# Projecting queries and keys of the sliding-block layers unpadded, through HBM, and setting constants later

## The chip, the cores and the metric

One core of one Trainium2 chip. The metric is the device time of one execution in microseconds (us); a kernel's time is the median of its runs. PE is the matmul engine, PEld its weight load, DVE VectorE, ACT ScalarE, POOL GpSimd, SP the engine from whose queue (SPq) most transfers are issued.

## The reference, cut to what matters

```python
# x: 1 x 2048 x 640; H = 32 heads of 20; W = 256
def _A_ref(x, wqkv, wo):                      # sliding-block attention
    qkv = (x @ wqkv).reshape(B, S, 3, H, Dh)...
    scores = einsum("bhqd,bhkd->bhqk", q, k) * (Dh ** -0.5)
    mask = (idx[:, None] - idx[None, :] >= 0) & (idx[:, None] - idx[None, :] < W)
    p = softmax(where(mask, scores, -1e9)); o = p @ v
    return o.transpose(...).reshape(B, S, D) @ wo
# _B_ref is the same without a mask: full attention
x = x + _A_ref(_layernorm(x), A_wqkv, A_wo)   # layer 1 (l = 0 in the code)
x = x + _B_ref(_layernorm(x), B_wqkv, B_wo)   # layer 2 (l = 1)
x = x + _A_ref(_layernorm(x), A_wqkv, A_wo)   # layer 3 (l = 2)
x = x + _B_ref(_layernorm(x), B_wqkv, B_wo)   # layer 4 (l = 3)
```

## The kernel before

The rows are cut into 4 chunks of 512, the heads into 8 groups of 4. A head has 20 columns, and the program computes its scores from a strip of 32 partitions of its own. The kernel had two ways to get there. The full layers (`l % 2 == 1`) project five blocks of 128 unpadded columns per chunk for queries and for keys, store them to HBM, and load each head's 20 rows back onto its strip. The sliding-block layers used weights with 12 zero columns after every 20, so that the projection itself lands on the strips; that takes eight projections instead of five, but no trip through HBM.

A scheduler in the program emits all engines' instructions "tile" by tile (a tile is one ScalarE exponential over two or three score banks); between tiles it advances waiting tasks (projections, normalization, statistics) by their need.

```python
def get_w(l, n, c, i):                       # weights of one projection
    t = wqkp.tile([P, KD, P], BF16, name="wqk", tag="wqk")
    wtick[l, n, c, i] = state["tick"] + 4     # may be used 4 tiles later
    if l % 2:                                 # full layer: unpadded, from the input
        a = n * D + i * P
        nc.sync.dma_start(out=t[:], in_=wq_view[1][:, :, a : a + P])
        return t
    d = wqk_d[i][:, n * KD * P : (n + 1) * KD * P]
    if l == 0 and c == 0:                     # pad once on chip, keep a copy in HBM
        ...
        nc.sync.dma_start(out=d, in_=t[:]...)
    else:
        nc.sync.dma_start(out=t[:]..., in_=d)
    return t

def t_qk_window(l, c, g):                     # sliding: straight onto the strips
    ...
    yield from project(wt, xnT[l, c], lambda: q[:])
    ...
    yield from project(wt, xnT[l, c], lambda: k[:])
    ready.add(("qk", l, c, g))

def t_full(l, n, c, b):                       # full: one block of 128, to HBM
    wt = yield from take_w(l, n, c, b)
    yield from project(wt, xnT[l, c], staged) # evicted into one of 4 staging tiles
    nc.sync.dma_start(out=dst, in_=staging.pop())
    ready.add(("qk"[n], l, c, b))
...
def keep_clock(least):                        # fillers
    while state["heat"] < least:
        t = choose(False)
        if t is not None and state["credit"] > -0.5:
            state["credit"] -= advance(t)     # real work first
            continue
        ...
        nc.tensor.matmul(ps[:, b, :], lhsT=ident[:], rhs=masks[:, 0, :], ...)
        state["heat"] += 1.0
...
def t_stats0(c):                              # layer 1's statistics of chunk c
    for i in range(4):
        stats(0, c, i)
        yield ("pe", 0.1)
    ready.add(("x", 0, c))
```

At the start, before any work:

```python
for t in (wop, *kts, *qts):                   # tiles whose unused rows must be zero
    nc.vector.memset(t[:], 0.0)
...
with tc.manual_schedule():
    other_constants()
    push("stats", t_stats0(0), 0, 0.4)
    push_layer(0, 0)
    require(("qk", 0, 0, 0))
```

The softmax here doesn't subtract the row's maximum and nothing guards it: scores larger than these inputs give would overflow.

Of the kernel before, what the change touches and what calls it, by code (L numbers as in the profile page):

```python
# [14 lines left out]
P = 128  # L15
# [6 lines left out]
G = 8  # L22
# [3 lines left out]
SCALE = DH ** -0.5  # L26
HD = D // 2
VW = DH + 1

PARTS = {  # L30
    l: [(e[n], e[n + 1]) for n in range(len(e) - 1)]
# [5 lines left out]
def kernel(  # L37
# [16 lines left out]
        return ctx.enter_context(tc.tile_pool(name=name, bufs=bufs, **kw))  # L54

    big = pool("big", 1)
    wqkp = pool("wqkp", 9)
    kvp = pool("kvp", 3)
    qap = pool("qap", 3)
    kap = pool("kap", 18)  # L60
    vap = pool("vap", 10)
    xtp = pool("xtp", 5)
    onp = pool("onp", 2)
# [26 lines left out]

    kts = [big.tile([P, S], BF16, name=f"kt{n}", tag=f"kt{n}") for n in range(3)]
    qts = [big.tile([P, C], BF16, name=f"qt{n}", tag=f"qt{n}") for n in range(4)]

    ps = psp.tile([P, 8, C], F32, name="ps", tag="ps")
    op = ps[:, 7, :]


    wqk_d = dram.tile([G, P, 2 * KD * P], BF16, name="wqk_d", tag="wqk_d")
    k_d = {l: dram.tile([D, S], BF16, name=f"k_d{l}", tag=f"k_d{l}") for l in (1, 3)}
    q_d = {l: dram.tile([NC, D, C], BF16, name=f"q_d{l}", tag=f"q_d{l}") for l in (1, 3)}  # L100
    v_d = {l: dram.tile([P, G, NT * 4 * VW], BF16, name=f"v_d{l}", tag=f"v_d{l}") for l in (1, 3)}

    wq_view = [w.rearrange("(c p) f -> p c f", p=P) for w in wqkv_in]
# [10 lines left out]
        for j in range(4):  # L114
            nc.sync.dma_start(out=wop[32 * j : 32 * j + DH, :, :], in_=v[j])

    for t in (wop, *kts, *qts):
        nc.vector.memset(t[:], 0.0)
    nc.gpsimd.memset(ident[:], 0.0)
    nc.gpsimd.affine_select(  # L120
        out=ident[:], in_=ident[:], compare_op=ALU.not_equal, fill=1.0,
# [2 lines left out]
    nc.gpsimd.memset(nhalf[:], -0.5)  # L124

    def other_constants():
        load_wop(0)
        nc.vector.memset(op, 0.0)
        nc.vector.tensor_copy(
            out=sel4[:], in_=ident[:].rearrange("p (j m) -> p j m", j=4)[:, :, DH]  # L130
        )

        sp32 = rzp.tile([32, 2, 16], BF16, name="sp32", tag="sp32")
        nc.vector.tensor_copy(
            out=sp32[:], in_=ident[0:32, 0:32].rearrange("p (n r) -> p n r", n=2)
        )
        sp16 = rzp.tile([32, 16], BF16, name="sp16", tag="sp16")
        nc.vector.tensor_tensor(out=sp16[:], in0=sp32[:, 0, :], in1=sp32[:, 1, :], op=ALU.add)
        nc.vector.tensor_copy(
            out=spread4[:].rearrange("p q (j m) -> p (q j) m", m=32),  # L140
            in_=sp16[:].unsqueeze(2).to_broadcast((32, 16, 32)),
        )

        nc.gpsimd.memset(masks[:], 1.0)
        for m, b, ge in (
            (2, 0, True), (2, 2, False), (2, 3, True),
            (0, 0, False), (0, 1, True), (0, 3, False),
            (1, 1, False), (1, 2, True),
        ):
            v = masks[:, m, b * P : (b + 1) * P]  # L150
            nc.gpsimd.affine_select(
                out=v, in_=v, compare_op=ALU.is_ge if ge else ALU.is_gt, fill=0.0,
                base=0, pattern=[[1 if ge else -1, P]], channel_multiplier=-1 if ge else 1,
            )
# [22 lines left out]
    def push(name, gen, need, left):  # L177
        lead = 0
        if type(name) is tuple and need <= first_use(1, NC - 1, 0):

            chain = {"out": True, "ln": name[1] == 1, "v": name[1] == 1 and name[-1] == 0}
            chain["k"] = chain["q"] = name[-1] == 0
            lead = 5 * chain.get(name[0], False)
        insort(todo, Task(name, gen, need, left, lead))

# [74 lines left out]


    live = Counter()
    cap = {"qa": 3, "ka": 18, "va": 10, "xnT": 5, "kt": 3, "vt": 3, "qt": 4, "ln": 1, "w": 4, "vs": 2}

    def room(*tags):
        while any(live[t] + tags.count(t) > cap[t] for t in tags):
# [24 lines left out]
    def get_w(l, n, c, i):  # L291

        t = wqkp.tile([P, KD, P], BF16, name="wqk", tag="wqk")
        wtick[l, n, c, i] = state["tick"] + 4
        if l % 2:
            a = n * D + i * P
            nc.sync.dma_start(out=t[:], in_=wq_view[1][:, :, a : a + P])
            return t
        d = wqk_d[i][:, n * KD * P : (n + 1) * KD * P]
        if l == 0 and c == 0:  # L300
            tv = t[:].rearrange("p c (j m) -> p c j m", j=4)
            nc.gpsimd.memset(tv[:, :, :, DH:32], 0.0)
            src = raw[:, :, n * D + 80 * i : n * D + 80 * (i + 1)]
            nc.vector.tensor_copy(
                out=tv[:, :, :, 0:DH], in_=src.rearrange("p c (j e) -> p c j e", j=4)
            )
            nc.sync.dma_start(out=d, in_=t[:].rearrange("p c m -> p (c m)"))
            wtick[l, n, c, i] = 0
        else:
            nc.sync.dma_start(out=t[:].rearrange("p c m -> p (c m)"), in_=d)  # L310
        return t

    def take_w(l, n, c, i):
# [46 lines left out]
    def t_ln(l, c):  # L360
# [3 lines left out]
        for n in (1, 0):  # L364
            order = worder[l, n]
            if order and not any(e in wtiles for e in order):
                wtiles[order[0]] = get_w(*order[0])
        users[l, c] = (9, 12, 9, 11)[l]
        mv = mvs.pop((l, c))
        rstd = lnp.tile([P, 4], F32, name="rstd", tag="rstd")  # L370
        nc.gpsimd.tensor_scalar(
# [89 lines left out]
    vt = {}  # L461
    qt = {}

    def t_qk_window(l, c, g):
        while ("xnT", l, c) not in ready:
            yield ("wait", 1)
        yield from room("qa", "ka", "w", "w")
        wt = yield from take_w(l, 0, c, g)
        q = qap.tile([P, C], BF16, name="qa", tag="qa")
        yield from project(wt, xnT[l, c], lambda: q[:])  # L470
        wt = yield from take_w(l, 1, c, g)
        k = kap.tile([P, C], BF16, name="ka", tag="ka")
        yield from project(wt, xnT[l, c], lambda: k[:])
        live["w"] -= 2
        qa[c, g], ka[c, g] = q, k
        used(l, c)
        ready.add(("qk", l, c, g))

    def t_full(l, n, c, b):

        while ("xnT", l, c) not in ready:
            yield ("wait", 1)
        yield from room("w")
        wt = yield from take_w(l, n, c, b)
        yield from project(wt, xnT[l, c], staged)
        rows = slice(b * P, (b + 1) * P)
        dst = k_d[l][rows, c * C : (c + 1) * C] if n else q_d[l][c, rows, :]
        nc.sync.dma_start(out=dst, in_=staging.pop())
        live["w"] -= 1
        used(l, c)  # L490
        ready.add(("qk"[n], l, c, b))
# [64 lines left out]
    def push_layer(l, c):  # L556
# [3 lines left out]
        if l % 2:  # L560
            halves = ((0,), (1,)) if l == 1 else ((0, 1),)
            for h in halves:
                push(("v", l, c, *h), t_v(l, c, h), need[4 * h[0]], 2.8 * len(h))
            for b in range(KD):
                g = b * P // 80
                for n in (1, 0):
                    worder[l, n].append((l, n, c, b))
                    first = need[g] if n else index[l, c, g, PARTS[l][0] if c == 0 else None]
                    push(("qk"[n], l, c, b), t_full(l, n, c, b), first, 1.1)
            return  # L570
        for g in range(G):
            for n in (0, 1):
                worder[l, n].append((l, n, c, g))
            push(("qk", l, c, g), t_qk_window(l, c, g), need[g], 2.2)
            if g == 0:
                push(("v", l, c), t_v(l, c, (0, 1)), need[0], 5.6)

# [80 lines left out]
                units.append(small.popleft())  # L658
    units += [Unit(3, 0, g, PARTS[3][1]) for g in range(G)]
    units += [Unit(3, c, g) for c in range(1, NC) for g in range(G)]  # L660
    full = [u for u in units if not u.windowed]
    place = {id(u): n for n, u in enumerate(full)}
    index = {(u.l, u.c, u.g, u.part): n for n, u in enumerate(units)}

    def first_use(l, c, g):
# [2 lines left out]
            return index[l, c, g, None]  # L668
        return next(index[l, 0, g, p] for p in PARTS[l] if 4 * c < p[1])

    def load_unit(u):

        l, c, g = u.l, u.c, u.g
        key = (l, c, g)
        k0, k1 = key_blocks(l, u.part)
        live["vt"] += 1
        vt[key] = kvp.tile([P, NT * 4 * VW], BF16, name="vt", tag="vt")
# [3 lines left out]
        )  # L681
        live["kt"] += 1
        live["qt"] += 1
        kt[key] = kts[len(loaded) % 3]
        qt[key] = qts[len(loaded) % 4]
        for j in range(4):
            rows = slice((4 * g + j) * DH, (4 * g + j + 1) * DH)
            strip = slice(32 * j, 32 * j + DH)
# [3 lines left out]

    def unit_needs(u):
        l, c, g = u.l, u.c, u.g
        if u.windowed:
            return [("qk", l, c, g)]
        k0, k1 = key_blocks(l, u.part)
        chunks = range(k0 // 4, k1 // 4)
        blocks = range(80 * g // P, (80 * g + 79) // P + 1)
        return [("q", l, c, b) for b in blocks] + [  # L700
            n
            for cc in chunks
# [5 lines left out]
    def ensure_loaded(u, force):  # L708
# [3 lines left out]
        if force:  # L712
            for n in needs:
                require(n)
        elif any(n not in ready for n in needs) or any(
            live[t] >= cap[t] for t in ("kt", "vt", "qt")
        ):
            return
        load_unit(u)
# [2 lines left out]
    def start_unit(u):  # L722
        for n in unit_needs(u):
            require(n)
        if not u.windowed:
            ensure_loaded(u, True)

    def load_ahead():

        for u in full:  # L730
            if id(u) not in loaded:
                ensure_loaded(u, False)
                return

    part_o = {}

# [26 lines left out]
    def s_emitted(u):  # L763
        if u.windowed:
            live["qa"] -= 1
            live["ka"] -= (u.c > 0) + (u.c == NC - 1)
        else:
            live["kt"] -= 1
            live["qt"] -= 1
# [55 lines left out]
        ready.add(("x", 0, c))  # L825

    with tc.manual_schedule():
        other_constants()
        push("stats", t_stats0(0), 0, 0.4)
        push_layer(0, 0)  # L830
        require(("qk", 0, 0, 0))

        def narrow(u):
# [163 lines left out]
```

## Time and profile before

| before | us |
|---|---|
| median of 4 runs | 2437.43 |
| lowest, highest | 2426.58, 2444.76 |
| span of the profiled run | 2436.6 |

The score matmuls (5504, the same in every kernel) serve as a ruler: a stage runs from one score matmul to another, whatever else lies between. "Half clock" is the time in which the throttle granted PE half its speed, summed from the clock records of the trace; it is the finer form of the mean clock that a view by stretches shows.

| stage, by scores | what runs | length before, us |
|---|---|---|
| to the first | start | 24.8 |
| first to 272nd | layer 1 alone | 127.6 |
| 272nd to 944th | layer 1, woven with early parts of layer 2 | 275.8 |
| 944th to 1088th | its last part | 71.7 |
| 1088th to 4000th | layers 2 and 4, layer 3 in between ("middle") | 1232.2 |
| 4000th to the end | layer 4 | 704.5 |

"The early stage" means first to 944th score from here on.

### The profile page before, as it was taken

What the parts mean: (1) busy time and instruction counts of PE and PEld (TensorE: products, weight loads), DVE (VectorE), ACT (ScalarE), POOL (GpSimd) and SP (SyncE); (2) the same over time, 40 slices, a digit from 0 to 9 for tenths busy, and PEclk for the clock granted to TensorE, in tenths of its full rate; (3) what the DMA queues carried; (4) which work ended last, traced back from release to release, by engine and by line L of the source; (5) the groups of instructions that cost most, each with busy time, mean ns of one, the idle gap of its engine ahead of it and who ended that gap; (6) DMA issues with size and microseconds to landing.
All of it is one profiled execution on the core that took longest, in us unless ns stands there. A gap on an engine that the chain in (4) does not pass through costs nothing.

```text
span 2436.6 us, 38927 instructions
## 1 busy us (share of the span) xinstructions
PE 2030.6 (83%) x15811; PEld 742.4 (30%) x15811; DVE 870.4 (36%) x1966; ACT 2234.2 (92%) x1779; POOL 39.8 (2%) x112
## 2 busy tenths in 40 slices
PE   6889899988888898888889888888877777777777
PEld 2333333323322333333322333332222222222222
DVE  6767767423323344433353434542200010001001
ACT  5878788899999999999998999999999999999997
POOL 2000000000000000000000000000000000000000
PEclk8999999999988999989997899999755575557556
DMA  4113223222100222102320032122100010010100
GB/s 149 58 43 83 64 61 91 54 75 75 47 24 26 48 66 67 39 13 56 83 67 16 16 89 74 31 46 62 58 28 26 25 36 26 25 36 31 33 13 12
DMA packets 141124, 120.19 MB, mean 49 GB/s; under 512 B 66064, under 2 KB 129680, under 8 KB 140944
## 3 DMA queue, kind: packets, MB, share of 16 engines
q1 hardware_dynamic: 140944, 117.70, 17.8%
q8 instruction: 124, 2.03, 0.3%
q14 instruction: 56, 0.46, 0.1%
HBM read 96.40 MB, written 21.23 MB: 48 GB/s over the span
## 4 chain that ended last, share of the span: by engine, by line
ACT 44%; PE 31%; issue 14%; DVE 10%; DMA 1%; SPq 0%; POOL 0%; ACTq 0%; DVEq 0%
ACT pt L903 44%; PE ps L337 8%; PE ps L889 7%; PE ps L953 4%; PE ps L510 4%; PE ps L588 3%; DVE pt L935 3%; PE ps L428 3%; DVE oT L760 1%; PE ps L392 1%; DVE st L283 1%; DVE ka L283 1%; DVE on L810 1%; DVE qa L283 1%; PE ps L806 1%
## 5 line engine op out<-in xcount | busy, mean ns | idle before, releaser
L903 ACT ACTIVATE pt<-ps 128x1536 bf16<-128x1536 f32 (+2 forms) x1704 | 2198.8, 1518 | 155.6 <-PE ps L889 132.3
L889 PE MATMUL ps<-qt,kt 32*128 32x512 bf16 x4096 | 667.7, 464 | 262.5 <-ACT pt L903 249.5
L953 PE MATMUL ps<-pt,vt 128*21 128x512 bf16 x4096 | 489.7, 465 | 11.1 <-DVE oT L760 7.6
L889 PEld LDWEIGHTS <-kt 32*128 32x128 bf16 x4096 | 202.1, 94 | 679.0 <-issue 656.8
L935 DVE TENSOR_TENSOR pt<-pt,masks 128x1024 bf16<-128x1024 bf16 (+5 forms) x403 | 240.4, 625 | 165.0 <-ACT pt L903 164.3
L337 PE MATMUL ps<-xnT,wqk 128*128 128x512 bf16 x1040 | 284.2, 400 | 16.8 <-DVE st L283 2.9
L760 DVE CAST oT<-ps 128x512 bf16<-128x512 f32 x112 | 76.8, 686 | 389.1 <-PE ps L953 389.0
L953 PEld LDWEIGHTS <-vt 128*21 128x21 bf16 x4096 | 106.2, 90 | 326.7 <-issue 316.5
L588 PE MATMUL ps<-masks,ident 128*128 128x512 bf16 x627 | 191.8, 419 | 11.9 <-DVE rz L787 3.0
L510 PE MATMUL ps<-wop,on 128*128 128x320 bf16 x968 | 174.5, 322 | 5.3 <-DVE x_sb L519 3.9
L810 DVE TENSOR_TENSOR on<-oT,ps 128x512 bf16<-128x512 bf16 x128 | 87.8, 686 | 153.2 <-PE ps L806 148.0
L889 PE MATMUL ps<-qa,ka 32*128 32x384 bf16 (+2 forms) x1408 | 118.1, 278 | 26.3 <-ACT pt L903 23.3
L519 DVE TENSOR_TENSOR x_sb<-x_sb,ps 128x320 bf16<-128x320 bf16 x120 | 58.0, 483 | 218.0 <-PE ps L510 217.7
L337 PEld LDWEIGHTS <-wqk 128*128 128x128 bf16 x1040 | 90.0, 100 | 140.8 <-issue 70.6
L428 PE MATMUL ps<-wv,xnT 128*128 128x320 bf16 x640 | 109.6, 303 | 4.0 <-DVE va L283 1.0
L510 PEld LDWEIGHTS <-on 128*128 128x128 bf16 x968 | 89.9, 103 | 73.6 <-issue 38.6
L953 PE MATMUL ps<-pt,va 128*21 128x384 bf16 (+2 forms) x1408 | 79.2, 291 | 21.7 <-DVE oT L760 16.0
L283 DVE CAST st<-ps 128x512 bf16<-128x512 f32 x78 | 53.9, 691 | 116.8 <-PE ps L337 111.0
L588 PEld LDWEIGHTS <-ident 128*128 128x128 bf16 x627 | 55.7, 103 | 96.4 <-issue 66.6
L799 DVE COPY rT<-ps 32x128 bf16<-32x128 bf16 x128 | 26.9, 210 | 143.3 <-PE ps L797 142.7
L787 DVE RECIPROCAL rz<-ps 128x16 f32<-128x16 f32 x128 | 32.7, 256 | 114.5 <-PE ps L782 113.5
L889 PEld LDWEIGHTS <-ka 32*128 32x128 bf16 x1408 | 40.1, 92 | 96.3 <-issue 91.0
(59 smaller groups left out, 778.8 us busy)
## 6 DMA issues: line engine op xcount, KB each, us to landing
wqk<-wqk_d SPq DMA_DIRECT2D x112, 160.0 KB
vt<-v_d SPq DMA_DIRECT2D x48, 336.0 KB
kt<-k_d SPq DMA_DIRECT2D x192, 80.0 KB
wqk<-in_B_wqkv_dram SPq DMA_DIRECT2D x80, 160.0 KB
qt<-q_d SPq DMA_DIRECT2D x384, 20.0 KB
v_d<-vs SPq DMA_DIRECT2D x16, 336.0 KB
k_d<-st SPq DMA_DIRECT2D x40, 128.0 KB
q_d<-st SPq DMA_DIRECT2D x40, 128.0 KB
```

Of the source, the lines that this page charges most:

```text
L283: nc.vector.tensor_copy(out=out_, in_=in_)
L337: nc.tensor.matmul(pq, lhsT=wt[:, dc, :], rhs=xt[:, dc, :], start=(dc == 0), stop=(dc == KD - 1),)
L428: nc.tensor.matmul(pv, lhsT=xt[:, dc, i * P : (i + 1) * P], rhs=wv_sb[l % 2][:, dc, h * HD : (h + 1) * HD], start=(dc == 0), stop=(dc == K ...
L510: nc.tensor.matmul(yp, lhsT=on[:, g, qb * P : (qb + 1) * P], rhs=wop[:, g, i * HD : (i + 1) * HD], start=(last or g == 0), stop=(g == G - 1),)
L519: nc.vector.tensor_tensor(out=xv, in0=had, in1=yp, op=ALU.add)
L588: nc.tensor.matmul(ps[:, b, :], lhsT=ident[:], rhs=masks[:, 0, :], start=True, stop=True)
L760: nc.vector.tensor_copy(out=oT[:], in_=op)
L810: nc.vector.tensor_tensor(out=on[:, g, :], in0=oT[:], in1=zb, op=ALU.mult)
L889: nc.tensor.matmul(sp[:, i, col * P : (col + qn) * P], lhsT=u.k(kc, j), rhs=u.q(j, q0, qn), start=True, stop=True,)
L903: nc.scalar.activation(out=pt[:, i:k, b0 * P :], in_=sp[:, i:k, b0 * P :], func=ACT.Exp, scale=SCALE,)
L935: nc.vector.tensor_tensor(out=pt_[:, i:k, b0 * P :], in0=pt_[:, i:k, b0 * P :], in1=mv_, op=ALU.mult,)
L953: nc.tensor.matmul(op[32 * j : 32 * j + VW, q0 * P : (q0 + qn) * P], lhsT=u.v(kc, j), rhs=pt[:, i, col * P : (col + qn) * P], start=(first ...
```

## The change

The sliding-block layers get their queries and keys as the full layers do, five unpadded blocks of 128 per chunk through HBM, in all chunks but layer 1's first. Per chunk that is 10 projections instead of 16. Key and query tiles of these layers become fixed tiles that are zeroed once (18 and 4, 22 new memsets), and all constants are set after the first statistics rather than ahead of them. The pool of weight tiles shrinks from 9 to 8.

```diff
-    for t in (wop, *kts, *qts):
-        nc.vector.memset(t[:], 0.0)
...
     def other_constants():
+        for t in (wop, *kts, *qts, *kas, *qas):
+            nc.vector.memset(t[:], 0.0)
...
-        if l % 2:
+        if l or c:
             a = n * D + i * P
-            nc.sync.dma_start(out=t[:], in_=wq_view[1][:, :, a : a + P])
+            nc.sync.dma_start(out=t[:], in_=wq_view[l % 2][:, :, a : a + P])
             return t
-        (copy of padded weights to and from HBM)
...
+        if c or l:                            # in push_layer
             for b in range(KD):
                 g = b * P // 80
                 for n in (1, 0):
...
+                    push(("qk"[n], l, c, b), t_block(l, n, c, b), first, 1.1)
...
+        if u.windowed:                        # in load_unit
+            ...
+            for j in range(4):
+                ...
+                nc.sync.dma_start(out=qa[c, g][strip, :], in_=q_d[l][c, rows, :])
+                nc.sync.dma_start(
+                    out=ka[c, g][strip, :], in_=k_d[l][rows, c * C : (c + 1) * C]
+                )
+            return
...
     with tc.manual_schedule():
-        other_constants()
         push("stats", t_stats0(0), 0, 0.4)
         push_layer(0, 0)
+        require(("x", 0, 0))
+        other_constants()
         require(("qk", 0, 0, 0))
```

## The prediction

> **What bounds the kernel now.** I read the page's busy shares first, then busy time by stage, then waits inside two stages, then the groups, then the first 25 us in order of time. ScalarE's exponentials lead over the whole span, but that average hides four stages, so I cut the span where the work changes: before the first score, the sliding-block layer 1 alone, layer 1 interleaved with early parts of full layer 2, the middle (rest of layer 2, layer 3 in between), and the last full layer.
>
> Busy time by stage: stretch, its length, then PE, weight loads, VectorE, ScalarE, GpSimd, granted clock, DMA share, GB/s:
>
> ```profile
> PE 2030.6 (83%) x15811; PEld 742.4 (30%) x15811; DVE 870.4 (36%) x1966; ACT 2234.2 (92%) x1779; POOL 39.8 (2%) x112
> ...
> 24.80:152.50 127.70, 110.43 (x1010) 50.48 (x1011) 92.65 (x234) 100.31 (x142) 9.22 (x23) 0.92 0.15 46
> 152.50:428.30 275.80, 251.36 (x2221) 101.06 (x2221) 192.47 (x408) 225.33 (x196) 5.88 (x14) 0.96 0.28 75
> 428.30:1732.10 1303.80, 1115.25 (x9082) 423.31 (x9080) 499.32 (x1107) 1228.08 (x934) 16.42 (x44) 0.93 0.20 52
> 1732.10:2436.60 704.50, 546.58 (x3484) 164.09 (x3480) 71.11 (x184) 675.48 (x502) 0.00 (x0) 0.57 0.09 27
> ```
>
> From 24.8 to 428 us PE is busy 86 to 91% and ScalarE 79 to 82%: PE leads. From 428 on ScalarE is busy 94 to 96%: it leads. Waits confirm the switch. First from 152.5 to 428.3, then from 428.3 to 1732.1 (engine and line, what ended the wait, us, times, longest):
>
> ```profile
> ACT pt L903 <- PE ps L889: 38.0, 57, 3.0
> ...
> PE ps L889 <- ACT pt L903: 2.2, 6, 0.7
> ```
>
> ```profile
> PE ps L889 <- ACT pt L903: 120.3, 286, 1.0
> ```
>
> Early, the exponentials wait for scores; later, scores wait for exponentials. So a saved PE microsecond counts early and hardly later. The groups concerned:
>
> ```profile
> L337 PE MATMUL ps<-xnT,wqk 128*128 128x512 bf16 x1040 | 284.2, 400 | 16.8 <-DVE st L283 2.9
> L588 PE MATMUL ps<-masks,ident 128*128 128x512 bf16 x627 | 191.8, 419 | 11.9 <-DVE rz L787 3.0
> ```
>
> L337 is the projection. L588 is filler: when queued PE work falls below a floor per score tile, the program inserts useless matmuls to hold the clock. The 400 ns mean is latency; in a run of five at full clock the pitch is 1.24 us / 5 = 0.25 us (0.44 us at the cold start, ten in 4.43 us).
>
> **What the Trainium skill says.** "TensorE: Matmul & The Clock Gate", Part 1 (The HAM clock gate): the PE clock is halved unless PE stays busy. The trace agrees: mean clock 0.96 in the packed stage, 0.57 in the last. That is why freed PE work will be refilled. "VectorE: DVE Perf Modes", Zero memsets can be issued as uint32 (trn2): a memset takes one cycle per element. The trace agrees in pitch: the 1024-word memsets start 1.07 us apart, the 256-word ones 0.27 us. "DMA: Bandwidth & Descriptors", Anatomy of one DMA: the issuing sequencer, not the DMA engine, waits on semaphores before dispatch, and completion into HBM is the larger part of a fixed cost of about 2 us (stated for the GpSimd path). The trace shows both for SP below. The same page's Specifications put line rate at 512 B per descriptor or more; the new weight loads have 256 B rows, as those of layers 2 and 4 have already, whose loads hold PE for only about 2 us in all.
>
> **The change, part by part.**
>
> 1) Projections. A sliding-block chunk needed 2 x 8 projections padded to 32 rows per head, and now 2 x 5 of unpadded 128 columns. Seven of eight chunks change: 7 x 6 x 5 = 210 matmuls and 42 evictions (0.69 us on VectorE) go. The instruction lists agree: 1040 to 830. But fillers rise from 627 to 768. Score matmuls are identical (5504), so I used them as a ruler through both lists. Up to the 944th (the end of the PE-led stages), projections go from 470 to 380 and fillers from 23 to 71; after it 570 to 450, and fillers 604 to 697. Early net: 90 x 0.25 = 22.5 us less, 48 x 0.25 = 12 us more, 10.5 us saved. By stretches the trade is uneven: before interleaving begins, layer-1 work moved forward makes PE about 5 us heavier; in the interleaved stage it gets about 14 to 15 us lighter, and ScalarE, at 42 to 44 us of each 49 to 60 us stretch, leaves room for it. I take -10. Later net: 120 out, 93 in, 27 x 0.27 = 7 us of PE where ScalarE leads; at under half on the path, -3.
>
> 2) Constants later. Intended: statistics first. Before:
>
> ```profile
> 1.40 2.19 DVE L118 MEMSET wop<- 128x2560 uint32 x1 [1.40 <-PEq L981]
> ...
> 6.82 1.09 DVE L118 MEMSET qt<- 128x256 uint32 x4
> ...
> 9.14 0.47 DVE L356 BATCH_NORM_STATS2 stats<-x_sb 128x6 f32<-128x320 bf16 x1
> ...
> 14.85 1.65 DVE L383 TENSOR_SCALAR xn<-x_sb,rstd,nmr 128x640 bf16<-128x640 bf16 x2
> ...
> 24.81 0.39 PE L889 MATMUL ps<-qa,ka 32*128 32x384 bf16 x6 [0.68 <-ACT ka L281]
> ```
>
> Constants take VectorE from 1.40 to 9.14, 7.7 us, largely while x is landing (both halves had by 4.7 us). In the new order statistics come first, from about 3.8 to 7.8 us, but all constants follow before the normalization that the first transpose needs, and 22 memsets of 256 words (the 18 key and 4 query tiles whose pad rows must be zero) are new: 22 x 0.272 = 6.0 us. Constants end at 7.8 + 7.7 + 6.0 = 21.5 us; two weight copies and one small operation later, normalization starts at 22.3 instead of 14.85, since the wait of 0.9 us for the reciprocal root is hidden. The first score moves from 24.8 to about 32.2: +7.4 us with nothing beside it.
>
> 3) Trips through HBM. 70 stores and 448 small loads join SP, 128 copies of padded weights become 70 loads from the input: 1540 issues become about 2050. SP takes about 0.34 us per small load (0.37 in pitch). It is not full, but in order, and a load right after its store blocks it:
>
> ```profile
> 161.00 0.33 SPq L488 DMA_DIRECT2D q_d<-st  x1
> 161.42 0.78 SPq L310 DMA_DIRECT2D wqk<-wqk_d  x1
> 162.29 0.38 SPq L678 DMA_DIRECT2D vt<-v_d  x1
> 163.89 0.31 SPq L689 DMA_DIRECT2D qt<-q_d  x1
> ```
>
> The store landed after 2.9 us, eight loads take 3 us more. Followed through the new order, the first two moved chunks have such triples every few score tiles, with the next weights and stores queued behind; weights are asked for only four tiles (some 6 us) ahead. I estimate two or three waits of 1 to 3 us in each of chunks 2 and 3 of layer 1: +7 in all. The loads themselves come five or more tiles ahead of use, so they are hidden. At the first unit of layer 2, which PE awaited 3.7 us in the kernel before, block 0 is now projected immediately ahead instead of a tile or two earlier: +2.5.
>
> 4) Smaller weight pool, copies of padded weights gone: nothing on the path.
>
> Sum: 7.4 + 7 + 2.5 - 10 - 3 = +3.9 us on 2437.4: 2441 us.
>
> **Rivals.** A: the saved PE time shows in full. For it: PE leads for 400 us and fillers may only fill gaps. If fillers cost nothing early (-22), SP never blocks and the start does not slip, the time is about 2410. Against it: in the stretches that lose most, ScalarE's 43 of 49 to 51 us leaves a floor some 5 us below. B: SP becomes a chain of its own. For it: VectorE or ScalarE evicts into four staging tiles that come free only when a store has landed, so one blocked load can stop eviction, then exponentials. If each of the 15 stored pairs of layer 1 costs 3 us, +45 on that part, about 2480. Against it: layer 2's stores and loads share this pattern already, and waits there on DMA sum to few microseconds. C: everything moved is hidden and only the start counts: about 2435 to 2445, not to be told from before by time alone.
>
> **Range and chances.** The start is nearly certain; the PE saving is good to 7 us, contention to 8, and the three runs of before spread by 18 us. Range 2421 to 2464. Over 2% is 49 us: reaching 2389 needs savings beyond what PE gives up early, chance 0.03; 2486 needs rival B in full, 0.05; within 2%, 0.92.
>
> **What would show it.** First score at about 32 us, VectorE memsets from about 8 to 20 us. 830 projections, 768 fillers. The 944th score about 1 to 10 us later than the 428.3 of before, though the stretch from the 272nd (152.5 us before) to it is about 10 us shorter. From there to the end within 6 us of before, with ScalarE's exponentials still at 2199 us. Waits of PE or evictions on weights or staging in the first 200 us growing from about 5 to some 10 us. I am wrong if the middle stage shrinks by over 15 us, or if DMA waits exceed 20 us, or if the first score comes as early as before.

## The result, and the profile after

The changed kernel takes 2466.05 us (2464.23 to 2467.37, four runs), against 2437.43. The ratio is 1.0121, with a 95% interval of 1.0082 to 1.0159. Such ratios are the mean time of one kernel's fast runs over that of the other's of the same rounds, so not quite the ratio of the medians. The time is above the predicted range, by 2 us.

| stage | before | after | difference | predicted |
|---|---|---|---|---|
| to the first score | 24.8 | 32.3 | +7.5 | +7.4 |
| first to 272nd | 127.6 | 139.0 | +11.4 | |
| 272nd to 944th | 275.8 | 293.9 | +18.1 | |
| first to 944th together ("early stage") | 403.4 | 433.0 | +29.6 | -10 + 7 + 2.5 = -0.5 |
| 944th to 1088th | 71.7 | 69.3 | -2.4 | |
| middle | 1232.2 | 1225.7 | -6.5 | |
| last | 704.5 | 705.0 | +0.5 | |
| after the 944th together | | | -8.4 | -3 |

The busy time of whole stretches of the kernel after, to be held against the prediction's block (stretch, length, then PE, weight loads, VectorE, ScalarE, GpSimd, granted clock, DMA share, GB/s):

```profile
PE 2025.8 (82%) x15742; PEld 741.4 (30%) x15742; DVE 847.2 (34%) x1939; ACT 2233.8 (91%) x1786; POOL 37.9 (2%) x112
...
32.28:171.40 139.12, 117.49 (x1045) 54.06 (x1046) 92.35 (x234) 103.71 (x151) 7.71 (x22) 0.91 0.19 48
171.40:465.30 293.90, 250.29 (x2144) 97.63 (x2144) 178.83 (x383) 222.23 (x194) 5.47 (x14) 0.91 0.29 76
465.30:1760.30 1295.00, 1102.31 (x9057) 421.88 (x9053) 485.01 (x1083) 1227.15 (x934) 16.40 (x44) 0.94 0.23 57
1760.30:2465.30 705.00, 548.75 (x3480) 164.32 (x3480) 71.06 (x183) 675.66 (x502) 0.00 (x0) 0.56 0.09 27
```

The second stretch holds 77 fewer matmuls than before, VectorE is 14 us and ScalarE 3 us less busy, and still it is 18 us longer, at a clock of 0.91 instead of 0.96. The early stage in one piece, before and after:

```profile
24.80:428.30 403.50, 361.78 (x3227) 151.54 (x3227) 285.12 (x642) 325.64 (x337) 15.10 (x37) 0.95 0.24 66
```

```profile
32.28:465.30 433.02, 367.79 (x3185) 151.70 (x3185) 271.18 (x617) 325.94 (x344) 13.18 (x36) 0.91 0.26 67
```

The 29.5 us split in two: PE is busy 6.0 us longer, with 42 fewer matmuls, and idle 23.5 us longer (65.2 us against 41.7). Half clock went from 44.4 to 78.5 us. The waits of the early stage say where the idle time lies (engine and line, what ended the wait, us, times, longest), before and then after; L337, L889 and L953 of before are L333, L914 and L978 of after (projection, scores, output of the attention):

```profile
ACT pt L903 <- PE ps L889: 48.1, 69, 3.0
...
PE ps L953 <- DVE oT L760: 7.5, 8, 2.6
...
PE ps L337 <- DMA wqk<-in_B_wqkv_dram: 1.4, 1, 1.4
```

```profile
ACT pt L928 <- PE ps L914: 78.9, 70, 10.3
...
PE ps L978 <- DVE oT L781: 13.9, 11, 5.0
...
PE ps L333 <- DMA wqk<-in_B_wqkv_dram: 10.4, 4, 3.0
PE ps L333 <- DMA wqk<-in_A_wqkv_dram: 10.0, 5, 4.0
...
PE ps L914 <- DMA kt<-k_d: 5.7, 4, 4.9
```

ScalarE waits 31 us longer for scores. Of PE's own waits, weights grew from 1.4 to 20.4 us in nine places, and the eviction of the attention's output from 7.5 to 13.9 us. So there are two suspects.

The first, in order of time around one weight wait of the kernel after (start, length, engine, line, operation; in brackets the idle time ahead of it and what ended it):

```profile
106.83 0.27 SPq L687 DMA_DIRECT2D qa<-q_d  x1
...
107.15 0.32 SPq L688 DMA_DIRECT2D ka<-k_d  x1
107.58 0.55 SPq L487 DMA_DIRECT2D k_d<-st  x1
...
108.23 0.38 SPq L487 DMA_DIRECT2D q_d<-st  x1
...
108.66 0.44 SPq L298 DMA_DIRECT2D wqk<-in_A_wqkv_dram  x1
...
111.30 1.04 PE L333 MATMUL ps<-xnT,wqk 128*128 128x512 bf16 x2 [4.01 <-DMA wqk<-in_A_wqkv_dram]
```

SP's transfers go out one after the other. The weights (L298) stand behind small loads and two stores; they go out at 108.66 and are there 2.6 us later. PE had stopped at 107.3.

The second, 50 us earlier in the same kernel:

```profile
56.86 0.47 DVE L352 BATCH_NORM_STATS2 stats<-x_sb 128x6 f32<-128x320 bf16 x1
...
60.73 0.21 DVE L354 BATCH_NORM_AGGREGATE mv<-stats 128x2 f32<-128x12 f32 x1
...
61.28 0.69 DVE L781 CAST oT<-ps 128x512 bf16<-128x512 f32 x1
...
62.02 0.61 PE L978 MATMUL ps<-pt,va 128*21 128x384 bf16 x8 [5.01 <-DVE oT L781]
```

The scheduler emits the statistics of a whole chunk at one point, four blocks of about 1 us, and in the new order the eviction that frees the output bank stands behind them. PE is idle 5.01 us.

At the start, the constants sit where the prediction put them:

```profile
8.63 2.19 DVE L127 MEMSET wop<- 128x2560 uint32 x1 [0.48 <-issue]
...
15.15 4.93 DVE L127 MEMSET ka<- 128x256 uint32 x18
20.08 1.09 DVE L127 MEMSET qa<- 128x256 uint32 x4
...
23.12 0.80 DVE L379 TENSOR_SCALAR xn<-x_sb,rstd,nmr 128x640 bf16<-128x640 bf16 x2
```

**Theory.** The late start costs 7.5 us; the rest is lost in the early stage, through layer 1 alone: weights late behind the new traffic in SP's queue (W), and statistics that block an eviction in the new order (S). **Rivals.** The weights are late because of their short rows, not because of the queue (R); the added fillers cost what the projections saved (F); the unpadded form is simply dearer wherever it is used (U). A fourth, that the weights are late because their pool has 8 tiles and not 9, was not named then; a_w_pool below, which keeps the 8, settles it.

### The profile page after: what moved, and what is told of

It reads as the page before. It is cut to its first block, busy times and chain, and to the rows that moved or that the text cites. A ratio compares the mean times of both kernels' runs of the same rounds, so it can differ in the third digit from the quotient of the medians.

```text
span 2465.3 us, 39504 instructions
## 1 busy us (share of the span) xinstructions
PE 2025.8 (82%) x15742; PEld 741.4 (30%) x15742; DVE 847.2 (34%) x1939; ACT 2233.8 (91%) x1786; POOL 37.9 (2%) x112
## 4 chain that ended last, share of the span: by engine, by line
ACT 44%; PE 30%; issue 15%; DVE 8%; DMA 2%; SPq 1%; POOL 0%; ACTq 0%; DVEq 0%
ACT pt L928 44%; PE ps L914 7%; PE ps L333 6%; PE ps L978 4%; PE ps L509 4%; PE ps L591 3%; PE ps L424 3%; DVE pt L960 2%; DVE st L284 1%; DMA wqk<-in_B_wqkv_dram 1%; DVE oT L781 1%; PE ps L388 1%; DVE on L834 1%; PE ps L830 1%; DVE x_sb L518 0%
## 5 line engine op out<-in xcount | busy, mean ns | idle before, releaser
L928 ACT ACTIVATE pt<-ps 128x1536 bf16<-128x1536 f32 (+2 forms) x1704 | 2196.4, 1511 | 173.5 <-PE ps L914 158.3
L914 PE MATMUL ps<-qt,kt 32*128 32x512 bf16 x4096 | 665.8, 463 | 274.0 <-ACT pt L928 258.2
L978 PE MATMUL ps<-pt,vt 128*21 128x512 bf16 x4096 | 488.5, 464 | 16.0 <-DVE oT L781 12.3
L914 PEld LDWEIGHTS <-kt 32*128 32x128 bf16 x4096 | 202.9, 94 | 685.8 <-issue 660.6
L333 PE MATMUL ps<-xnT,wqk 128*128 128x512 bf16 x830 | 229.3, 403 | 31.7 <-DMA wqk<-in_B_wqkv_dram 11.3
L591 PE MATMUL ps<-masks,ident 128*128 128x512 bf16 x768 | 233.4, 416 | 6.8 <-DVE st L284 2.5
L978 PEld LDWEIGHTS <-vt 128*21 128x21 bf16 x4096 | 106.0, 90 | 333.4 <-issue 322.3
L284 DVE CAST st<-ps 128x512 bf16<-128x512 f32 x133 | 91.9, 691 | 218.6 <-PE ps L333 204.9
L914 PE MATMUL ps<-qa,ka 32*128 32x384 bf16 (+2 forms) x1408 | 119.7, 283 | 30.2 <-ACT pt L928 26.8
L424 PE MATMUL ps<-wv,xnT 128*128 128x320 bf16 x640 | 115.0, 315 | 6.2 <-DVE on L834 2.4
L333 PEld LDWEIGHTS <-wqk 128*128 128x128 bf16 x830 | 71.8, 100 | 131.1 <-issue 52.6
L591 PEld LDWEIGHTS <-ident 128*128 128x128 bf16 x768 | 68.0, 102 | 114.2 <-issue 76.8
L978 PE MATMUL ps<-pt,va 128*21 128x384 bf16 (+2 forms) x1408 | 79.7, 291 | 18.4 <-DVE oT L781 15.4
L914 PEld LDWEIGHTS <-ka 32*128 32x128 bf16 x1408 | 41.0, 93 | 101.9 <-issue 95.2
```

What stands on the lines that cost most here:

```text
L284: nc.vector.tensor_copy(out=out_, in_=in_)
L333: nc.tensor.matmul(pq, lhsT=wt[:, dc, :], rhs=xt[:, dc, :], start=(dc == 0), stop=(dc == KD - 1),)
L424: nc.tensor.matmul(pv, lhsT=xt[:, dc, i * P : (i + 1) * P], rhs=wv_sb[l % 2][:, dc, h * HD : (h + 1) * HD], start=(dc == 0), stop=(dc == K ...
L914: nc.tensor.matmul(sp[:, i, col * P : (col + qn) * P], lhsT=u.k(kc, j), rhs=u.q(j, q0, qn), start=True, stop=True,)
L928: nc.scalar.activation(out=pt[:, i:k, b0 * P :], in_=sp[:, i:k, b0 * P :], func=ACT.Exp, scale=SCALE,)
L978: nc.tensor.matmul(op[32 * j : 32 * j + VW, q0 * P : (q0 + qn) * P], lhsT=u.v(kc, j), rhs=pt[:, i, col * P : (col + qn) * P], start=(first ...
```

## The experiments

In the table, "stage" is the early stage and "half" the half clock in it, both from each kernel's one profile; time against before is the ratio, times 2437, less 2437.

| run | median (range), us | ratio to before, 95% | against before, us | first score | stage | half |
|---|---|---|---|---|---|---|
| before | 2437.4 | 1 | 0 | 24.8 | 403.4 | 44.4 |
| after | 2466.1 | 1.0121 (1.0082 to 1.0159) | +29.5 | 32.3 | 433.0 | 78.5 |
| a_w_pool | 2440.9 (2427.6 to 2446.1) | 1.0018 (0.9973 to 1.0064) | +4.4 | 32.5 | 407.9 | 47.8 |
| a_loads_pool | 2444.4 (2436.3 to 2451.9) | 1.0035 (0.9997 to 1.0074) | +8.5 | 32.0 | 410.1 | 54.6 |
| a_stats_spread | 2445.9 (2444.2 to 2446.3) | 1.0046 (1.0013 to 1.0079) | +11.2 | 32.1 | 419.0 | 64.9 |
| b_stats_spread | 2436.8 (2433.4 to 2442.5) | 1.0007 (0.9980 to 1.0034) | +1.7 | 24.8 | 400.7 | 27.3 |
| a_const_off | 2460.5 (2451.0 to 2472.5) | 1.0111 (1.0054 to 1.0167) | +27.1 | 20.1 | 438.8 | 68.3 |
| a_const_dve | 2453.1 (2447.3 to 2455.1) | 1.0066 (1.0044 to 1.0089) | +16.1 | 20.7 | 432.9 | 71.7 |
| b_const_late | 2445.9, one run, state unknown | - | (+8.4) | 32.5 | 402.0 | 37.5 |
| a_nofill_early | 2462.0 (2456.7 to 2463.8) | 1.0105 (1.0080 to 1.0130) | +25.6 | 32.1 | 425.3 | 108.1 |
| l2_only | 2429.5 (2426.3 to 2432.8) | 0.9975 (0.9951 to 1.0000) | -6.1 | 32.0 | 405.9 | 37.5 |
| l1_only | 2469.6 (2466.0 to 2473.6) | 1.0138 (1.0116 to 1.0161) | +33.6 | 31.4 | 428.5 | 61.4 |
| combo_l2 | 2432.5 (2425.2 to 2448.0) | 0.9991 (0.9963 to 1.0019) | -2.2 | 21.0 | 410.6 | 34.1 |
| combo_all | 2419.7 (2411.9 to 2427.9) | 0.9938 (0.9913 to 0.9962) | -15.1 | 22.0 | 404.7 | 51.2 |

All gave right results. Three cautions. By the intervals of the two rows, a difference between a repair and the kernel after is uncertain by 11 to 17 us. One profile is one execution: stretches whose code is the same in two kernels differ by up to 9 us between profiles (b_const_late has before's code in the middle stage and took 1241.4 us there against 1232.2). And some traces lack matmul records (a_w_pool's shows 3150 matmuls but 3183 weight loads in the early stage), so PE's busy time is compared only between traces whose two counts agree.

### a_w_pool: the weights leave SP's queue

```diff
-            nc.sync.dma_start(out=t[:], in_=wq_view[l % 2][:, :, a : a + P])
+            nc.gpsimd.dma_start(out=t[:], in_=wq_view[l % 2][:, :, a : a + P])
```

PE's instructions and their order are as in the kernel after; only the 150 weight loads are issued from GpSimd.

> The changed kernel with only the 150 weight loads of 128 columns issued from GpSimd instead of SP; the order on PE is the same, instruction by instruction. Theory Q (weights are late because they stand behind small loads and stores in SP's in-order queue): PE's waits on weights fall from about 21 us before the 944th score to under 6, half-clock time there falls from 78 to under 60 us, and the stage from first to 944th score from 433 to about 405 us; time about 2440. Rival R (256-byte rows are slow to land, whoever issues them): waits on weights stay at 15 us or more and the time at 2460 or above. Rival D (GpSimd's own in-order queue or its slower issue delays weights as much): weights still awaited, GpSimd shown busy or waiting.

The time falls by 25 us against the kernel after, and the early stage by 25.1. Early-stage waits of this run:

```profile
ACT pt L928 <- PE ps L914: 61.6, 67, 11.3
...
PE ps L978 <- DVE oT L781: 14.1, 11, 5.0
...
PE ps L914 <- DMA kt<-k_d: 6.5, 2, 6.2
```

No wait of PE on weights is left in the list, while the waits on the eviction are where they were (13.9 us before the edit). The pool still has 8 tiles, so its size did not make the weights late. W is shown. The profile fell on the fastest of the four runs (2427.6 us): its span is 40 us below that of the kernel after, where the times differ by 25, and its middle stage is 9 us shorter as well, so the 25.1 us of the early stage flatter the move somewhat.

### a_loads_pool: the small loads leave SP's queue instead

```diff
-                nc.sync.dma_start(out=qa[c, g][strip, :], ...)
-                nc.sync.dma_start(out=ka[c, g][strip, :], ...)
+                nc.gpsimd.dma_start(out=qa[c, g][strip, :], ...)
+                nc.gpsimd.dma_start(out=ka[c, g][strip, :], ...)
```

> The changed kernel with the 448 small query and key loads of the sliding-block layers issued from GpSimd, everything else on SP; same order on PE. Theory Q: SP's queue is short again, weights come in time: waits of PE on weights before the 944th score from about 21 us to under 8, that stage from 433 to 405-415 us, time 2438 to 2448. Rival S (it is the stores, not the small loads, that hold the weights up): waits on weights stay above 14 us. Rival P (small loads on the other queue arrive late themselves): new waits on query or key loads of more than 5 us.

Here the weights stay on SP with their rows of 256 B, and the 448 small loads move. The time falls by 21 us. PE's waits on weights in the early stage fall from 20.4 to 4.4 us:

```profile
PE ps L333 <- DMA wqk<-in_B_wqkv_dram: 2.7, 2, 2.4
...
PE ps L333 <- DMA wqk<-in_A_wqkv_dram: 1.7, 1, 1.7
```

Short rows are thus not what made them late (R falls): either party may leave the queue, and the lateness goes. GpSimd's queue now waits many times before it may overwrite a query tile, once 33.1 us, and the list of PE's waits shows no new one on query or key loads.

### a_stats_spread and b_stats_spread: one block of statistics per tile

```diff
         for i in range(4):
             stats(0, c, i)
             yield ("pe", 0.1)
+            yield ("wait", 1)
```

> The changed kernel with the statistics of layer 1's later chunks given out one row block per score tile instead of four (12 VectorE instructions, 4 us) at once. Theory B (a burst ahead of the eviction of the attention output stops PE twice, 5.0 and 4.0 us, and costs the clock after it): the gaps at about 57 and 250 us go, the stage from first to 944th score shortens by 8 to 16 us, time 2450 to 2458. Rival (bursts only take the place of a wait that comes anyway, as the kernel before has the same bursts): under 4 us.

> The kernel before with layer 1's statistics given out one row block per score tile. If the burst stops PE there as well (gaps of 2.6, 2.2 and 3.0 us at about 102, 48 and 244 us), the stage to the 944th score shortens by 4 to 10 us, time 2426 to 2433. If the spreading helped the changed kernel only because its bursts fell ahead of evictions, under 3 us here.

On the kernel after this saves 18 us of time and 14.0 us of the early stage; on the kernel before it changes nothing that the times can tell (1.0007, interval 0.9980 to 1.0034). The code of the statistics is the same in both. It is the order around them that the change made worse: in the old order no bank of the output waited behind them for long. The waits of PE in the early stage after the edit (L979 is L978 of the kernel after):

```profile
PE ps L333 <- DMA wqk<-in_B_wqkv_dram: 10.2, 6, 3.7
PE ps L979 <- DVE oT L781: 10.0, 8, 2.5
...
PE ps L333 <- DMA wqk<-in_A_wqkv_dram: 6.8, 3, 4.6
```

The longest wait on the eviction falls from 5.0 to 2.5 us, but the sum only from 13.9 to 10.0; the waits on weights fall from 20.4 to 17.0 us and half clock from 78.5 to 64.9. That the bursts cost this time in the new order is shown (S); how much of it goes through the eviction, and how much through the clock and the shifted order, was not taken apart. S was not in the prediction at all.

b_stats_spread has a second lesson: half clock fell from 44.4 to 27.3 us and the stage only by 2.7. Half clock is not lost time by itself.

### b_const_late: the old kernel with the constants late

```diff
-    for t in (wop, *kts, *qts):
-        nc.vector.memset(t[:], 0.0)
...
     def other_constants():
+        for t in (wop, *kts, *qts):
+            nc.vector.memset(t[:], 0.0)
+        for n in range(22):
+            nc.vector.memset(qts[n % 4][:], 0.0)
...
-        other_constants()
         push("stats", t_stats0(0), 0, 0.4)
         push_layer(0, 0)
+        require(("x", 0, 0))
+        other_constants()
```

> The kernel before with one part of the change alone: constants set after the first statistics, and 22 memsets of 256 words more (of tiles that are zeroed anyway). Theory (VectorE's order alone makes the start): first score at 32.2 us plus or minus 0.3 instead of 24.8, and the rest as before, about 2445 us. Without the 22 memsets it would be 26.2. Rival (the start needs the HBM trips or the missing copies of padded weights): first score well below 32.

2445.87 us. The stand-in memsets and the first score, in order of time:

```profile
15.58 6.03 DVE L128 MEMSET qt<- 128x256 uint32 x22
...
32.46 0.39 PE L892 MATMUL ps<-qa,ka 32*128 32x384 bf16 x6 [0.68 <-ACT ka L283]
```

22 memsets take 6.03 us and the first score comes at 32.46, 0.2 us from that of the kernel after. The early stage keeps its length (402.0 us). The start's 7.5 us is what the constants cost, and the 402.0 us show no catching up; this is one profile of one run.

### a_const_off and a_const_dve: the zeros leave the start

```diff
# a_const_off: all in one place, 18 tiles in, on GpSimd
+    def pad_zeros():
+        for t in (*kas[8:], *kts, *qts, wop):
+            nc.gpsimd.memset(t[:], 0.0)
+        load_wop(0)
...
+            if t == 18:
+                pad_zeros()
# a_const_dve: on VectorE, one per tile
+    pads = deque((*kas[8:], *kts, *qts, wop))
...
+            if t >= 6 and pads:
+                nc.vector.memset(pads.popleft()[:], 0.0)
+                if not pads:
+                    load_wop(0)
```

(Eight key tiles and the query tiles are first used by chunk 0, whose padded projection writes every row, so only the later ones need zeros, and not at once.)

> The changed kernel with its pad zeroing off the start: the memsets of the key, query and output-weight pads go to GpSimd, 18 score tiles in; the eight key tiles and four query tiles that the first chunk overwrites whole are not zeroed. Theory (constants ahead of the normalization are the whole of the later start): first score at about 21 us instead of 32.3, since only 1.2 us of constants and the landing of the raw weights (11.2 us) remain; time about 11 us below the changed kernel, 2455, and everything after the start as long as in the changed kernel. Rival (the start slips for other reasons, or the memsets on GpSimd hold up its other work): first score above 25 us, or the gain lost again by the 272nd score.

> The changed kernel with its pad zeroing taken off the start, now on VectorE, one memset in each score tile from the seventh on (18 memsets). First score at about 20 us as in a_const_off, no gap of 10.6 us, since VectorE is never held while GpSimd writes: the first 272 scores take 136 to 141 us and the time is 2451 to 2456, 10 to 14 below the changed kernel. Rival (memsets in VectorE's stream cost as much there as at the start): 2460 or more.

In both the first score comes 11.6 to 12.2 us earlier than in the kernel after. a_const_off hardly gains from it: the time falls by 2 us, within its interval, and its rival comes true, since the 272nd score comes at 171.7 us as in the kernel after (171.3). A new stop appears where GpSimd writes zeros:

```profile
54.70 12.81 DVE L817 CAST hl<-rz 128x16 bf16<-128x16 f32 x1
55.41 5.30 POOL L127 MEMSET kt<- 128x2048 bf16 x3
...
60.65 1.93 POOL L127 MEMSET qt<- 128x512 bf16 x4
62.52 4.36 POOL L127 MEMSET wop<- 128x5120 bf16 x1
...
67.78 0.29 PE L823 MATMUL ps<-ident,hl 128*32 128x128 bf16 x1 [10.64 <-DVE hl L818]
```

A VectorE cast of 16 columns, 0.17 us at its next use (76.65), takes 12.81 us, until GpSimd has ended a chain of memsets without a pause (the eight shown, and four short ones up to 67.49 us), and PE loses 10.64 us. The Trainium skill, "SBUF - State Buffer", section "Who interferes with whom", has VectorE's two-port copies and casts and GpSimd share one pair of ports, which whoever issues first holds for the whole instruction. The direction agrees; but the cast was held through more than eight instructions, not one, and earlier in the same chain, at 52.03 us, a VectorE copy of 400 columns went through in 0.36 us. That the ports are the cause was not tested.

a_const_dve avoids that, and the time falls by 13 us, as much as the first score came earlier plus 2. Its early stage stays at 432.9 us, so the start and the early stage are independent costs.

### a_nofill_early: no fillers before the interleaved part of layer 2 is full

```diff
+            if state["unit"] >= index[1, 0, 0, PARTS[1][3]]:
                 nc.tensor.matmul(ps[:, b, :], lhsT=ident[:], rhs=masks[:, 0, :], ...)
             state["heat"] += 1.0
```

> The changed kernel with the 71 filler matmuls before the 944th score left out (697 instead of 768 in all), all else in the same order. If fillers cost their full PE time there, as the prediction booked them (0.25 us each), the stage shortens by up to 17 us; if they only fill gaps where ScalarE leads, it stays within 5 us; if they do hold the clock, half-clock time rises from 78 us and the stage gets longer by 3 us or more. I expect within 5 us, time 2460 to 2470.

The edit removes 107 fillers (71 before the 944th score, 36 up to the 1088th); the expectation put the count lower. The early stage is 7.7 us shorter though half clock rises from 78.5 to 108.1 us, so the expectation that it would stay within 5 us missed. The time is only 4 us below the kernel after, with overlapping intervals. 71 fillers are about 18 us of PE at 0.25 us each; less than half of that comes back. F is a quarter of the stage's loss at most (7.7 of 29.6 us), and no gain from the fillers in this stage shows either.

### l2_only and l1_only: which layer loses

```diff
# l2_only: layer 1 as in before, layer 3 unpadded
-        if l or c:
+        if l:
# l1_only: layer 1 unpadded, layer 3 as in before
-        if l or c:
+        if l % 2 or (l == 0 and c):
# (and the same condition in push_layer, unit_needs, start_unit; padded weights
#  kept in HBM again for the padded layer)
```

Both keep the late constants.

> The changed kernel with layer 1 as in the kernel before (padded projections into the tiles for all its chunks, weights copied through HBM) and only layer 3 projected unpadded through HBM; late constants stay. Theory (all the loss is in layer 1's HBM traffic and in the start): first score at 32.3, the stage to the 944th score as before, 403 plus or minus 4 us, the middle stage 1288 to 1297 us instead of 1304: time 2434 to 2442. Rival (the middle stage gains nothing, its 9 us are the scatter of one profile): 2443 to 2449.

> The complement of l2_only: layer 1 unpadded through HBM, layer 3 padded as in the kernel before; late constants stay. If the parts add, this has the late start (+7.4), the long early stage (+26 to +30) and none of the middle stage's gain: middle stage from the 1088th to the 4000th score 1232 to 1241 us, time 2473 to 2482. If the two layers' parts act on each other (weight pool, queue), it lies elsewhere.

l2_only is 6 us faster than before while it starts 7.2 us later: unpadding layer 3 is worth 13 us. l1_only is 34 us slower than before, a little less than expected, 27 us without its late start (6.6 us). U falls: the same change gains in one layer and loses in the other. The two don't quite add: 33.6 - 6.1, less the start counted twice (about 7), is about +20, against the measured +29.5. The 9 us between lie inside the intervals (6, 6 and 9 us to either side), so no interaction is shown and none is excluded.

### combo_l2 and combo_all: the repairs together

combo_l2 is l2_only with the zeros spread on VectorE and the statistics spread; combo_all is the kernel after with the weights from GpSimd, the zeros spread on VectorE and the statistics spread.

```diff
# combo_all: the edits of a_w_pool, a_const_dve and a_stats_spread
# combo_l2:  the edits of l2_only, a_const_dve and a_stats_spread
```

> Layer 3 alone unpadded, plus zeroing spread and statistics spread. From l2_only's 2429.5: 12 less for the start, 0 to 6 for the statistics: 2412 to 2418. If it equals combo_all, unpadding layer 1 is worth nothing even when its weights come in time; if it is over 5 us faster, unpadding layer 1 costs; if over 5 us slower, it gains.

> The changed kernel with three repairs: weights issued from GpSimd, pad zeroing spread over score tiles on VectorE, statistics spread. If the causes are separate they add: 2466 less 25, 12 and 8 to 20 gives 2410 to 2421, under the kernel before by 0.7 to 1.1%. If they overlap (the same clock windows counted twice), about 2428.

combo_all takes 2419.7 us, ratio 0.9938 (0.9913 to 0.9962): it beats both kernels. combo_l2, expected at 2412 to 2418, takes 2432.5 and misses: its first score comes 11.0 us earlier than l2_only's, but by the profiles 6 us of that are lost again up to the 1088th score, and its six runs scatter by 23 us; the cause was not sought. combo_all is 13 us (plus or minus 9) faster than combo_l2 (0.9991 - 0.9938, of 2437), so unpadding layer 1, which costs 27 us as it stands, shows no cost any more once its weights come in time. That it gains is not shown. The difference carries the weights' move with it, and the move alone on combo_l2 was not run; by the profiles only 5.9 us of it lie in the early stage, where layer 1 runs, and 7.9 us in the middle stage, where it is over.

The three repairs save 25, 18 and 13 us each by themselves, 57 in sum, and 45 together; the 12 us between lie inside the intervals. The early stages point to an overlap, from one profile each: the weights' move takes 25.1 us off, the spread statistics 14.0, both 28.3. The early stage of combo_all, by busy time:

```profile
22.10:426.80 404.70, 350.62 (x3163) 148.74 (x3163) 282.25 (x642) 322.89 (x337) 66.61 (x98) 0.94 0.28 75
```

## Why the prediction was wrong, and where it was right

**Bound, start and counts: right.** PE leads to the 944th score, ScalarE after; ScalarE's exponentials took 2196.4 us (2198.8 before). The first score came at 32.3 us for "about 32.2", and b_const_late shows the whole of it in the constants. That it fits so closely is partly luck: normalization began at 23.12 us, not at 22.3, and most of the 0.8 us between was made up before the first score. 830 projections and 768 fillers are in the trace.

**Step 1, projections, early: right in kind, not visible in the time.** Predicted -10 us. Three traces with complete records share PE's work of the kernel after and differ in half clock: 78.5, 71.7 and 61.4 us of it go with 367.8, 364.1 and 361.5 us of busy PE. By that slope (0.37) an estimate for before's 44.4 us of half clock is 355 us, 6.5 us under before's 361.8. combo_all, which needs 22 fillers fewer, is busy 350.6 us at 51.2 us of half clock, 11.2 us under before. The work was saved. But even there the stage is 404.7 us long against 403.4: what PE saves, it waits. The saving was put on the path as a whole, and the runs show no shortening of this stage from it.

**Step 3, trips through HBM: the mechanism was named, the size was not.** This is the step that failed. It allowed +7 us for two or three waits of 1 to 3 us in each of two chunks. The trace has nine waits of up to 4.0 us on weights, 20.4 us for 1.4 before, and taking them away by either of two means brings 21 to 25 us. The prediction's own sign of being wrong, waits on DMA above 20 us, came true. I looked for the blockage at the load that follows its own store, as in the kernel before. That wait is rare after the change (2.2 us in all for SP in the early stage). What delays the weights is in large part the mere length of what stands ahead: a group's eight loads take about 3 us of issuing, and such groups come in a row. In the 7 us ahead of the late weights, seven of the nine cases have eight or more of the new query and key loads. Loads that the kernel before has as well add to it. Ahead of the wait that ends at 214.3 us SP issued fifteen small loads of layer 2 and one of values without a pause from 205.0 to 211.0 us, then a store, and only at 211.5 the weights, which had been asked for just four tiles ahead:

```profile
205.03 0.33 SPq L709 DMA_DIRECT2D kt<-k_d  x1
...
210.66 0.33 SPq L709 DMA_DIRECT2D kt<-k_d  x1
211.09 0.34 SPq L487 DMA_DIRECT2D k_d<-st  x1
211.53 0.40 SPq L298 DMA_DIRECT2D wqk<-in_B_wqkv_dram  x1
```

Length is not all. In the 14 us before, ahead of seven of the nine, the queue had also stood still at least once for 1 us or more, for an eviction or for a tile not yet free; the two shares were not separated. The count of SP's issues in this step, 1540 to about 2050, took in instructions that move nothing: the traces have 1232 and 1692 transfers, the 460 more that the step's own parts give. Rival B named SP as a chain of its own and said 2480; it was nearer than the sum, but by luck: it put the loss in the staging tiles, and evictions hardly wait on them (two waits on a transfer, 4.1 and 3.0 us, in the early stage).

**A wait that no step had.** The statistics burst ahead of the eviction (5.0 us at 57 us, again 4.0 us at 250 us) is made by the new order of work. Every rival considered what was added to queues; none asked which old instructions would change places. Spreading it is worth 18 us after the change and nothing that the times can tell before it.

**The clock.** The prediction filled freed PE time with fillers but put no price on a gap beyond its length. After the change, gaps of over 1.2 us sum to 34.6 us (14.4 before), and 34 us more of half clock came with them; by the slope above, which is an estimate from three profiles, the slower clock turns a saving in PE's work into 6 us more of busy time. That two repairs share this cost may be why they don't add up; it was not shown. It is not a cost that half clock has everywhere: b_stats_spread and a_nofill_early changed it by 17 and 30 us with little or the opposite effect on the stage.

**The first unit of layer 2: right in sign, half the size.** Its wait for keys went from 3.7 to 4.9 us, for a predicted +2.5.

**Later stages: right in sign, too small.** Predicted -3 us. The middle stage took 1235.4 us on average in the four profiled kernels whose layer 3 is padded (1231.3 to 1241.4) and 1222.0 in the ten others (1214.1 to 1225.7), and l2_only's time says 13 us as well. The estimate took under half of 7 us of PE. What else is saved there (ScalarE waits for scores or VectorE's evictions) was not taken apart, so the mechanism of this gain is open.

**The sum.** Start +7.5 for +7.4; early stage +29.6 for -0.5; the rest -8.4 for -3. The range failed by its early stage alone.

## What to carry to other kernels

Count what a change adds to a queue that issues in order, by when each request is due: a queue with idle time still delivers late if a prefetch stands behind a batch, and moving either party to another queue can be the whole repair of that wait. When work is removed or moved in a kernel that a scheduler orders, look through the new order for long bursts on an engine ahead of the short instruction that another engine awaits. A change that loses as a whole may hold a gain: here halves, by layer, and repairs one at a time, found a version 0.6% faster than the start.

## What the Trainium skill lacked or had wrong

- "SBUF - State Buffer", "Who interferes with whom", speaks of a lock held for one instruction. Here one VectorE cast of 16 columns took 12.81 us (0.17 us otherwise) while GpSimd ran memsets back to back until 67.49 us, eight of them from 55.4 to 66.9 us; yet a copy of 400 columns passed in 0.36 us at 52.03, earlier in the same run of memsets. The cause was not isolated.
- "TensorE: Matmul & The Clock Gate", "HAM oscillation - how this bites in real kernels", gives gaps of over about 3.4 us as what it calls the abstract rule for falling back to half clock. In the kernel after, gaps of 3.0, 2.9 and 2.4 us (ending at 339.3, 406.2 and 424.6 us) were followed within 1.5 us by 3.4 to 6.8 us of half clock, and half clock from 387.1 us on (6.8 us) had no gap of over 0.9 us in the 6 us before it. So the length of the last gap does not decide alone here. That half-clock periods come in multiples of about 3.4 us (3.4, 6.8, 10.2, 13.7) agrees with Part 1 of the page.
- "DMA: Bandwidth & Descriptors" gives no time for what SP pays to issue a small load on this chip; its one figure per instruction, in sequencer cycles for "previous generations", stands in a passage on another chip. Here it is 0.27 to 0.33 us (0.37 us from one to the next), 3 us for the eight of a head group, and this, far more than bytes, made weights late: the DMA share was 0.24 before and 0.26 after in the early stage.
- No page says how long issuing the same load holds GpSimd and how long SP: a weight load held GpSimd for 0.87 us and SP for 0.43 us (medians of 150, a_w_pool and the kernel after). The 62 of them that fall in the early stage took GpSimd from 13 to 66 us of busy time there, and the kernel got 25 us faster.
